# Joined exponentials and moved score groups in a windowed-attention kernel with a ReLU-squared feed-forward behind it

## The chip, the core and the metric

One Trainium2 chip, one of its cores. The metric is the device time of one execution in microseconds (us). TensorE (PE in the profile) multiplies matrices into PSUM, which has eight banks; ScalarE (ACT) evaluates functions, here exponentials, ReLU and copies; VectorE (DVE) works elementwise; GpSimd (POOL) casts and issues loads; SyncE (SP) issues the other transfers. Each engine runs its own instructions in program order and waits on semaphores for the others.

## The reference, cut to what matters

```python
# q, k, v: (8 batch rows, 8 heads, 576 tokens, 64)
rel = pos[:, None] - pos[None, :]
mask_plain = (rel >= 0) & (rel < 32)                      # heads 0 to 3
mask_dil = (rel >= 0) & (rel < 128) & (rel % 4 == 0)      # heads 4 to 7
scores = where(masks, q @ k.T / sqrt(64), -1e9)
attn_out = softmax(scores) @ v
x = attn_out.transpose(0, 2, 1, 3).reshape(4608, 512)
h = x @ w_in            # (512, 2048)
r = maximum(h, 0.0)
out = (r * r) @ w_out   # (2048, 512)
```

## The kernel before

The attention goes by batch row (0 to 7, 576 tokens each), the feed-forward by chunk (0 to 8, 512 tokens each). While the feed-forward of chunk c runs on TensorE, the attention of row c + 1 is strewn between its matmuls. `run` (L861) does this by hand-written plans such as `"7:s34"`: the feed-forward is a generator, `pump(n)` advances it by n steps, and the part named behind the colon is issued after that many steps of the chunk.

A chunk from 2 on has 60 steps. Steps 1 to 32 are the first multiplication and ReLU: 16 tiles with two steps each, a step being two matmuls (L295) of 512 columns, then a ReLU on ACT (L304) and a square on DVE (L329). Steps 33 to 60 are the second multiplication, done for chunks 2 to 8 with seven block products instead of eight (`seven_gen`, L462): four steps for each product, a step being four matmuls (L447) of 256 columns. In this text they are products 1 to 7. Products 1, 2, 3, 5 and 6 end with a copy or sum that takes the result out of its banks: after 3 ACT copies it to `u2` (L514), after each half of 5 to `t7` (L521), after 6 to the output tile (L528). After product 4, DVE computes `S4` in place of S1 (two L433, through `sum_g`), and after product 5 it adds `pc` and `t7` (L523). Product 7 reads S4 and adds on top of `pc`, the banks of product 4. In chunks 0 and 1 the second multiplication is a plain one (L336), two 512-wide matmuls to a step.

The attention of a row has these parts:

- scores in three groups of two kinds each: kinds 0 to 2 are the windowed heads, kinds 3 to 5 the dilated ones. From row 2 on the groups are `s34`, `s50` and `s12` (row 1: `s01`, `s23`, `s45`). A group (`scores`, L641) issues its matmuls (L660, 64 rows by 72 or 96 columns) into two pairs of banks, an exponential of each kind on ACT (L671), and masks on DVE: L675 one mask for a group of two windowed kinds, L682 and L688 one for each kind of the others.
- `a0` to `a2` (windowed) and `d0`, `d1`, `e0`, `e1` (dilated): probabilities times values (L753, L783) into one pair of banks, then a reciprocal and a normalization on DVE (L733, L734).
- `x0`, `x1`, `y0`, `y1`: transposes on TensorE (L805, L820) and copies on ACT into `xr`, the input of the feed-forward (L812, L823). From row 5 on transfers transpose instead; `w0` and `w1` then copy the dilated part into place on ACT (L831).

The pairs are banks 4 and 5 (pair 2) and banks 6 and 7 (pair 3), taken in turn by `pair()` (L84, `turns["pair"]`); the feed-forward uses banks 0 to 3. Each row from 2 on takes an odd number of turns, so the pair on which a row begins alternates. `d0` is the first to take a pair after `s12`.

Chunk 0's second multiplication carries row 1 (L1078). The plans for later rows are `SOON` for the scores, `EARLY` for the rest, and `LATER`, whose second part places the scores of row c + 2 behind chunk c's first multiplication, for c = 3 to 5: `s34` at step 40, `s50` at 47 (behind three quarters of product 4), `s12` at 54 (the middle of product 6). Row 4's groups stand at step 58 of chunk 2 and at steps 2 and 5 of chunk 3, and its `d0` at step 8; row 3's `s12` and `d0` at steps 17 and 21 of chunk 2; row 2's at steps 34 and 40 of chunk 1.

Of the kernel before, what the change touches and what calls it, by code (L numbers as in the profile page):

```python
# [12 lines left out]
ACTF = mybir.ActivationFunctionType  # L13
P = 128
# [3 lines left out]
def kernel(  # L18
# [9 lines left out]
    nc = tc.nc  # L28
# [10 lines left out]
    scale = float(1.0 / (D ** 0.5))  # L39
# [6 lines left out]
    QB = 96  # L46
# [27 lines left out]
    PS = pspool.tile([P, 8, TOKC], FP32, name="PS")  # L74
    turns = {"bank": 0, "pair": 0}
# [8 lines left out]
    def pair(dt=FP32):  # L84
        i = pairs[turns["pair"] % len(pairs)]
        turns["pair"] += 1
        b = PS[:, 2 * i : 2 * i + 2, :]
        return b if dt == FP32 else b.bitcast(dt)
# [36 lines left out]
    AT = const.tile([P, 5120], FP16, name="AT")  # L125
# [7 lines left out]
    maskp = const.tile([P, 2 * 4 * QB], FP16, name="maskp")  # L133
# [23 lines left out]
    def load_whole_sliding_qk(b):  # L157
        n = natp.tile([P, HH, 9, D], FP16, name=f"n{b}", tag="n")
        for i, s in ((1, k), (0, q)):
            nc.gpsimd.dma_start(  # L160
                out=n[64 * i : 64 * (i + 1)],
                in_=s[b, 0:HH].rearrange("h (p j) d -> p h j d", j=9),
            )
        return n
# [85 lines left out]
    def keep_dilated_qk(b):  # L250
        d = dpool.tile([2, HH * CL, DIL * D], FP16, name=f"dd{b}", tag="dd")
        for i, src in ((1, k), (0, q)):
            nc.gpsimd.dma_start(
                out=d[i], in_=src[b, HH:H].rearrange("h (i c) d -> (h i) (c d)", c=DIL)
            )
        return d
# [333 lines left out]
    def t_sliding(b, n, hp):  # L590
        p_ = pair(FP16)
        for i in (1, 0):
            t_sliding_one(b, n, hp, 2 * hp, i, p_[:, i, :])
        for i in (1, 0):
            c_sliding_one(b, hp, i, p_[:, i, :], nc.vector if i else nc.scalar)
# [16 lines left out]
    def t_dilated(b, m, a):  # L612
        p_ = pair(FP16)
        for i in (1, 0):
            t_dilated_one(b, m, a, i, p_[:, i, :])
        for i in (1, 0):
            c_dilated_one(b, a, i, p_[:, i, :], nc.vector if i else nc.scalar)
# [9 lines left out]
    def dilated_of(base, n):  # L627
        return AT[:, base : base + 2 * n * QX].rearrange("p (e n q) -> p e n q", e=2, q=QX)
# [5 lines left out]
    def place_of(block, e):  # L634

        for base, blocks in KINDS:
            if block in blocks:
                w = QB if len(block) == 2 else QX
                return base + w * (e * len(blocks) + blocks.index(block))

    def scores(b, *kinds):  # L641

        tiles = [pair() for i in kinds]
        for i, ps in zip(kinds, tiles):
            for n, block in enumerate(KINDS[i][1]):
                if i < 3:
                    m, hp = block
                    kk = QKTp[b % 2][:, 1, hp, QB * m : QB * m + P]
                    qq = QKTp[b % 2][:, 0, hp, PADP + QB * m : PADP + QB * (m + 1)]
                    w = QB  # L650
                else:
                    t, a, h = block
                    q0 = KPAD + h * CL + QD * t
                    k0 = q0 - (PADE if t else PADD)
                    kk = QKTd[b % 2][:, 1, a, k0 : k0 + P]
                    qq = QKTd[b % 2][:, 0, a, q0 : q0 + QD]
                    w = QD
                for e in range(2):
                    r = slice(D * e, D * (e + 1))
                    nc.tensor.matmul(  # L660
                        ps[:, e, w * n : w * (n + 1)], kk[r], qq[r], start=True, stop=True
                    )
        for i, ps in zip(kinds, tiles):
            base, blocks = KINDS[i]
            n = len(blocks)
            if i < 3:
                to, of = AT[:, base : base + 2 * n * QB], ps[:, :, 0 : n * QB]
            else:
                to = dilated_of(base, n)[:, :, :, 0:QD]
                of = ps[:, :, 0 : n * QD].rearrange("p e (n q) -> p e n q", q=QD)  # L670
            nc.scalar.activation(to, of, ACTF.Exp, scale=scale)  # L671
        if max(kinds) < 3:
            i0, n = kinds[0], len(kinds)
            x = AT[:, 800 * i0 : 800 * (i0 + n)].rearrange("p (i w) -> p i w", w=800)[:, :, 0 : 8 * QB]
            nc.vector.tensor_mul(x, x, maskp.unsqueeze(1).to_broadcast([P, n, 8 * QB]))  # L675
            return
        for i in kinds:
            base, blocks = KINDS[i]
            n = len(blocks)
            if i < 3:  # L680
                x = AT[:, base : base + 2 * n * QB]
                nc.vector.tensor_mul(x, x, maskp)  # L682
                continue

            o = QD * (0, 4, 6)[i - 3]
            mask = maskd.rearrange("p t w -> p (t w)")[:, o : o + n * QD]
            x = dilated_of(base, n)[:, :, :, 0:QD]
            nc.vector.tensor_mul(  # L688
                x,
                x,  # L690
                mask.rearrange("p (n q) -> p n q", q=QD).unsqueeze(1).to_broadcast([P, 2, n, QD]),
            )
# [143 lines left out]
    def row_parts(b, wide):  # L836

        xs, ys, zs = [], [], []
        return {
            "s01": lambda: scores(b, 0, 1),  # L840
            "s23": lambda: scores(b, 2, 3),
            "s45": lambda: scores(b, 4, 5),
            "s34": lambda: scores(b, 3, 4),
            "s50": lambda: scores(b, 5, 0),
            "s12": lambda: scores(b, 1, 2),
            "a0": lambda: av_sliding(b, xs, 0, 1),
            "a1": lambda: av_sliding(b, xs, 2, 3),
            "a2": lambda: av_sliding(b, xs, 4, 5),
            "x0": lambda: b < CROSS and x_sliding(b, 0, xs, wide),
            "x1": lambda: b < CROSS and x_sliding(b, 1, xs, wide),  # L850
            "d0": lambda: av_dilated(b, 0, 0, ys),
            "d1": lambda: av_dilated(b, 0, 1, ys),
            "e0": lambda: av_dilated(b, 1, 0, zs),
            "e1": lambda: av_dilated(b, 1, 1, zs),
            "y0": lambda: b < CROSS and x_dilated(b, 0, ys, wide),
            "y1": lambda: b < CROSS and x_dilated(b, 1, zs, wide),
            "w0": lambda: place_dilated(b, 0),
            "w1": lambda: place_dilated(b, 1),
        }
# [125 lines left out]
    s01 = pair()  # L985
# [18 lines left out]
    for u in (5, 7):  # L1004
        x = AT0[:, u, 0:UW].rearrange("p (e w) -> p e w", e=2)
# [46 lines left out]
    n, dd = load_whole_sliding_qk(2), keep_dilated_qk(2)  # L1052
# [5 lines left out]
    def turn(b, n, dd):  # L1058
# [5 lines left out]
        if b < 4:  # L1064
# [6 lines left out]
        t0=lambda: t_sliding(1, ns1, 0),  # L1071
        t1=lambda: t_sliding(1, ns1, 1),
        u0=lambda: t_dilated(1, nd1, 0),
        u1=lambda: t_dilated(1, nd1, 1),
    )
    run(
        (
            "1:t0 3:t1 6:s01 8:u0 10:u1 12:a0 14:a1 15:s23 17:x0 18:s45 20:a2 22:d0 24:x1"  # L1078
            " 25:d1 26:e0 28:e1 29:y0 30:y1",
            parts,  # L1080
        ),
# [9 lines left out]
    rows_ = {b: row_parts(b, b > SEVEN) for b in range(2, B)}  # L1091
    SOON = "{}:s34 {}:s50 {}:s12"
    EARLY = "{}:d0 {}:d1 {}:e0 {}:y0 {}:e1 {}:a0 {}:y1 {}:a1 {}:a2 {}:x0 {}:x1"
    LATER = (EARLY.format(2, 5, 8, 11, 13, 16, 19, 21, 24, 27, 30), SOON.format(40, 47, 54))
    PLANS = {
        1: (SOON.format(24, 29, 34) + " " + EARLY.format(*range(40, 62, 2)), ""),
        2: (
# [4 lines left out]
            "2:s50 5:s12 " + EARLY.format(8, 11, 14, 17, 19, 22, 24, 27, 30, 33, 36),  # L1102
            LATER[1],
        ),
        4: (LATER[0] + " 57:w0 60:w1", LATER[1]),
        5: (LATER[0] + " 57:w0 60:w1", LATER[1]),
        6: (LATER[0] + " 57:w0 60:w1", ""),
    }

    ORDER = {1: 46, 2: 33, 3: 9, 4: 2, 5: 2}  # L1110
    for c in range(1, NTOKC):
        b = c + 1
# [10 lines left out]
        if b + 1 < B:  # L1123
# [4 lines left out]
            n, dd = load_whole_sliding_qk(b + 1), keep_dilated_qk(b + 1)  # L1128
# [53 lines left out]
```

## Time and profile before

| | |
|---|---|
| runs before | 298.99, 298.40, 298.44 us; median 298.44 |
| profiled execution | 297.93 us, of which 295.6 is the span from first to last instruction |
| TensorE clock granted | full, the whole span |
| VectorE, ScalarE, GpSimd busy | 203.6, 176.5, 97.3 us of the span |
| transfers | DMA engines 9 tenths busy or more in most slices up to about 207 us, 3 tenths or less after it |

The profile shows one execution. Times in its timeline count from the first instruction. Chunk 3 runs from about 120 to 152 us, chunk 4 to 182, chunk 5 to 212; chunks 6 to 8, which carry less and less attention, to 292. Row 1 stands at 36 to 58 us. Matmuls are pipelined: a row "x8" counts eight, its length includes the pipeline's tail of the last one. A weight load (PEld) runs beside the matmul before it. Where an engine stood idle, brackets behind the row give the time and what ended it. "issue" there is time in which the profile shows no wait.

### The profile page before, as it was taken

To read this page: it belongs to the slowest core of one execution; us is meant where nothing else is said; L and a number is where in the kernel's file an instruction comes from. 1 tells how busy PE (TensorE), PEld (TensorE's weight loads), DVE (VectorE), ACT (ScalarE), POOL (GpSimd) and SP (SyncE) were. 2 spreads that over 40 slices of the span, in tenths; PEclk is the share of its full clock that TensorE was granted. 3 is DMA by queue.
4 is the path that set the end of the run, shared out by engine and by line. 5 is a ranking of instruction groups with operands and counts; after the bars stand their busy time and mean duration, and the time that the engine had idled before them with its cause. 6 is when DMAs were issued, how large, how long until landed. Compare 5 with 4: busy or idle time off the path is not lost.

```text
span 295.6 us, 7127 instructions
## 1 busy us (share of the span) xinstructions
PE 285.0 (96%) x2880; PEld 202.5 (69%) x2880; DVE 203.6 (69%) x381; ACT 176.5 (60%) x318; POOL 97.3 (33%) x154
## 2 busy tenths in 40 slices
PE   3989999999999999999999999999999999999995
PEld 2769855565555588557889987568756875785584
DVE  7786656778735997799588958896779524823652
ACT  2678855779438773886645557655756267425711
POOL 8591029406707113951563029309300000000000
PEclk9999999999999999999999999999999999999999
DMA  7999999599899698999999999999223130003013
GB/s 124 240 200 211 213 207 200 160 176 234 161 217 252 140 167 163 237 233 168 205 252 222 175 156 224 240 179 149 79 87 38 26 144 0 0 2 143 2 35 106
DMA packets 73968, 45.58 MB, mean 154 GB/s; under 512 B 56720, under 2 KB 67600, under 8 KB 73744
## 3 DMA queue, kind: packets, MB, share of 16 engines
q1 hardware_dynamic: 66544, 31.37, 48.0%
q0 software_dynamic: 7248, 13.63, 26.0%
q8 instruction: 22, 0.36, 0.5%
q10 hardware_dynamic: 144, 0.13, 0.1%
q14 instruction: 10, 0.08, 0.1%
HBM read 36.83 MB, written 16.52 MB: 180 GB/s over the span
## 4 chain that ended last, share of the span: by engine, by line
PE 83%; DVE 6%; ACT 3%; DMA 3%; issue 2%; SPq 1%; POOL 1%; POOLq 0%; DVEq 0%; ACTq 0%
PE PS L295 40%; PE PS L447 23%; PE PS L336 9%; PE PS L783 2%; PE PS L660 2%; ACT AT L671 2%; DVE S L433 2%; DMA nd<-in_q_dram 2%; PE PS L753 2%; PE PS L577 1%; DMA sv<-in_v_dram 1%; PE PS L805 1%; SPq L172 1%; PE PS L601 1%; PE PS L820 1%
## 5 line engine op out<-in xcount | busy, mean ns | idle before, releaser
L295 PE MATMUL PS<-xr,wi 128*128 128x512 f16 (+3 forms) x704 | 133.3, 341 | 0.3
L304 ACT ACTIVATE rt<-PS 128x512 f16<-128x512 f32 (+2 forms) x160 | 87.9, 557 | 40.8 <-PE PS L295 37.8
L295 PEld LDWEIGHTS <-wi 128*128 128x128 f16 x704 | 75.9, 113 | 38.6 <-issue 0.4
L329 DVE TENSOR_TENSOR g<-rt 128x1024 f16<-128x1024 f16 (+1 forms) x64 | 46.1, 721 | 28.0 <-ACT rt L304 27.6
L447 PEld LDWEIGHTS <-S 128*128 128x128 f16 x448 | 43.0, 98 | 6.4 <-issue 1.1
L671 ACT ACTIVATE AT<-PS 128x768 f16<-128x768 f32 (+2 forms) x42 | 31.8, 810 | 13.7 <-PE PS L660 13.5
L447 PE MATMUL PS<-T,S 128*128 128x256 f16 x336 | 39.0, 273 | 0.0
L447 PEld LDWEIGHTS <-g 128*128 128x128 f16 x336 | 32.3, 98 | 5.1
L336 PE MATMUL PS<-wo,g 128*128 128x512 f16 x128 | 32.9, 379 | 0.0
L239 POOL CAST vd<-sd 128x512 f16<-128x512 f32 x32 | 24.8, 796 | 19.8 <-DMA sd<-in_v_dram 16.7
L222 POOL CAST vp<-sv 128x512 f16<-128x512 f32 x24 | 18.2, 760 | 24.9 <-DMA sv<-in_v_dram 23.8
L447 PE MATMUL PS<-wo,g 128*128 128x256 f16 x224 | 26.3, 273 | 0.0
L688 DVE TENSOR_TENSOR AT<-AT,maskd 128x720 f16<-128x720 f16 (+1 forms) x21 | 14.0, 678 | 14.0 <-ACT AT L671 13.7
L734 DVE TENSOR_TENSOR y<-PS,rcp 72x512 f16<-72x512 f32 (+1 forms) x32 | 22.0, 686 | 1.1
L734 DVE TENSOR_TENSOR x<-PS,rcp 96x512 f16<-96x512 f32 (+1 forms) x25 | 16.6, 665 | 0.9
L783 PEld LDWEIGHTS <-AT 128*128 128x128 f16 x256 | 12.1, 100 | 6.4 <-DVE y L734 1.4
L433 DVE TENSOR_TENSOR S<-g,S 128x1024 f16<-128x1024 f16 x14 | 11.5, 860 | 6.9 <-PE PS L447 6.9
L336 PEld LDWEIGHTS <-g 128*128 128x128 f16 x128 | 10.4, 97 | 8.2
L226 POOL CAST vp<-sv 32x512 f16<-32x512 f32 (+1 forms) x24 | 15.0, 626 | 1.5
L733 DVE RECIPROCAL rcp<-PS 96x8 f32<-96x8 f32 (+3 forms) x57 | 11.2, 197 | 5.4 <-PE PS L753 2.7
L447 PE MATMUL PS<-wo,S 128*128 128x256 f16 x112 | 13.5, 272 | 0.6 <-DVE c L523 0.5
L447 PE MATMUL PS<-T,g 128*128 128x256 f16 x112 | 14.1, 273 | 0.0
(101 smaller groups left out, 287.0 us busy)
## 6 DMA issues: line engine op xcount, KB each, us to landing
out_dram<-c SPq DMA_DIRECT2D x12, 512.0 KB
sv<-in_v_dram SPq DMA_DIRECT2D x48, 96.0 KB, 3.9
sd<-in_v_dram SPq DMA_DIRECT2D x16, 288.0 KB
dp<-o SPq DMA_DIRECT2D x12, 288.0 KB, 3.9
wo<-in_moe_w_out_dram POOLq DMA_DIRECT2D x4, 512.0 KB, 13.9
n<-in_k_dram POOLq DMA_DIRECT2D x6, 288.0 KB, 6.0
n<-in_q_dram POOLq DMA_DIRECT2D x6, 288.0 KB, 6.9
dd<-in_k_dram POOLq DMA_DIRECT2D x6, 288.0 KB, 7.6
```

The costliest lines, as they stand in the source:

```text
L222: nc.gpsimd.tensor_copy(vp[b % 2][:, m : m + 2, :, 0:D], sv[:, m : m + 2, :, :])
L226: nc.gpsimd.tensor_copy(vp[b % 2][0:PADP, m:m1, :, 0:D], sv[P - PADP : P, m - 1 : m1 - 1])
L239: nc.gpsimd.tensor_copy(o, by_class(sd[:, t]))
L295: nc.tensor.matmul(ph[:, o : o + b - a], w_in_of(dmk, ffc), xr[:, dmk, a:b], start=(dmk == 0 and o == 0), stop=(dmk == NDM - 1 and o + b - ...
L304: nc.scalar.activation(rt, ph[:, 0:w], ACTF.Relu)
L329: nc.vector.tensor_mul(g[:, f2 : f2 + 2, o:TOKC], rt[:, :, o:TOKC], rt[:, :, o:TOKC])
L336: nc.tensor.matmul(po, g[:, ffc, o + t * P : o + (t + 1) * P], w_out_of(ffc), start=(ffc == 0), stop=(ffc == NFF - 1),)
L433: nc.vector.tensor_sub(S1[:, f, :], a_of(0, 1, j), S2[:, f, :])
L447: nc.tensor.matmul(po[t], lhs(j)[:, t * P : (t + 1) * P], rhs(j), start=j == 0 and not on_top, stop=j == HF - 1, skip_group_check=on_top,)
L671: nc.scalar.activation(to, of, ACTF.Exp, scale=scale)
L734: nc.vector.tensor_tensor(out=x, in0=pv[:, :, :, 0:D], in1=rcp[0:w, 0:i, 0:j].unsqueeze(3).to_broadcast([w, i, j, D]), op=ALU.mult,)
L783: nc.tensor.matmul(pav[:, e, h * (D + 2) : h * (D + 2) + D + 1], AT[:, off : off + P], vd[b % 2][:, t, 2 * a + e, h, 0 : D + 1], start=Tru ...
```

## The change

Three edits. In `scores`, for groups of windowed kinds from row 2 on (`s12`), the two exponentials of 128 by 768 become one of 128 by 1536 that reads the four banks 4 to 7; before such a group the turn of pairs is made even, so that the group begins on banks 4 and 5, and one turn is skipped where it was odd. The mask behind it is the same instruction as before. In `LATER`, `s50` goes from step 47 to step 45 (the first quarter of product 4 in front of it, three behind it). In row 1's plan `s23`, `x0`, `s45` and `a2` go one step later; `d0`, `x1` and all after them stay. The number of instructions falls by six on ACT and stays on the other engines.

```diff
+    def two_sliding(i):
+        x = AT[:, 800 * i : 800 * (i + 2)].rearrange("p (i w) -> p i w", w=800)
+        return x[:, :, 0 : 8 * QB]
+
     def scores(b, *kinds):
 
+        if b > 1 and max(kinds) < 3:
+
+            turns["pair"] += turns["pair"] % 2
         tiles = [pair() for i in kinds]
...
+        if b > 1 and max(kinds) < 3:
+
+            nc.scalar.activation(
+                two_sliding(kinds[0]).rearrange("p i (e w) -> p i e w", e=2),
+                PS[:, 4:8, 0 : 4 * QB].rearrange("p (i e) w -> p i e w", e=2),
+                ACTF.Exp,
+                scale=scale,
+            )
+            tiles = []
         for i, ps in zip(kinds, tiles):
...
         if max(kinds) < 3:
-            i0, n = kinds[0], len(kinds)
-            x = AT[:, 800 * i0 : 800 * (i0 + n)].rearrange("p (i w) -> p i w", w=800)[:, :, 0 : 8 * QB]
-            nc.vector.tensor_mul(x, x, maskp.unsqueeze(1).to_broadcast([P, n, 8 * QB]))
+            x = two_sliding(kinds[0])
+            nc.vector.tensor_mul(x, x, maskp.unsqueeze(1).to_broadcast([P, 2, 8 * QB]))
             return
...
-            "1:t0 3:t1 6:s01 8:u0 10:u1 12:a0 14:a1 15:s23 17:x0 18:s45 20:a2 22:d0 24:x1"
+            "1:t0 3:t1 6:s01 8:u0 10:u1 12:a0 14:a1 16:s23 18:x0 19:s45 21:a2 22:d0 24:x1"
             " 25:d1 26:e0 28:e1 29:y0 30:y1",
...
-    LATER = (EARLY.format(2, 5, 8, 11, 13, 16, 19, 21, 24, 27, 30), SOON.format(40, 47, 54))
+    LATER = (EARLY.format(2, 5, 8, 11, 13, 16, 19, 21, 24, 27, 30), SOON.format(40, 45, 54))
```

## The prediction

> **What bounds the kernel now.** I read first the page's busy shares and its chain, for the engine that sets the end; then the timelines around each edit, for where that engine stands still.
>
> ```profile
> PE 285.0 (96%) x2880; PEld 202.5 (69%) x2880; DVE 203.6 (69%) x381; ACT 176.5 (60%) x318; POOL 97.3 (33%) x154
> PE 83%; DVE 6%; ACT 3%; DMA 3%; issue 2%; SPq 1%; POOL 1%; POOLq 0%; DVEq 0%; ACTq 0%
> ```
>
> TensorE (PE) is busy for 96% of the span and carries 83% of the chain, so an edit is worth what it takes from PE's standing time, no more. ScalarE (ACT) has 40% of the span free, so its own savings buy nothing by themselves. The largest stop that comes back is one wait per chunk in the second half of chunks 3, 4 and 5. Chunk 4:
>
> ```profile
> 174.14 0.59 ACT L514 COPY u<-PS 128x512 f32<-128x512 f32 x1 [0.46 <-PE PS L447]
> ...
> 175.52 0.34 PE L660 MATMUL PS<-QKTp 64*128 64x96 f16 x8
> 175.73 1.47 ACT L671 ACTIVATE AT<-PS 128x720 f16<-128x720 f32 x2 [1.00 <-PE PS L660]
> 175.79 2.36 PE L447 MATMUL PS<-T,S 128*128 128x256 f16 x20
> ...
> 177.23 0.71 DVE L682 TENSOR_TENSOR AT<-AT,maskp 128x768 f16<-128x768 f16 x1 [0.17 <-ACT AT L671]
> ...
> 177.87 2.11 DVE L433 TENSOR_TENSOR S<-g,S 128x1024 f16<-128x1024 f16 x2
> ...
> 178.18 0.37 ACT L521 COPY t<-PS 128x256 f32<-128x256 f32 x1 [0.50 <-PE PS L447]
> ...
> 178.95 0.51 PE L660 MATMUL PS<-QKTp 64*128 64x96 f16 x16
> 179.34 1.51 ACT L671 ACTIVATE AT<-PS 128x768 f16<-128x768 f32 x2 [0.78 <-PE PS L660]
> ...
> 179.40 1.05 PE L447 MATMUL PS<-T,g 128*128 128x256 f16 x8
> 179.90 0.68 DVE L523 TENSOR_TENSOR c<-PS,t 128x512 f32<-128x512 f32 x1
> ...
> 180.63 1.91 PE L447 MATMUL PS<-wo,S 128*128 128x256 f16 x16 [0.19 <-DVE c L523]
> ...
> 180.74 0.59 ACT L528 COPY c<-PS 128x512 f32<-128x512 f32 x1
> ...
> 181.20 2.49 ACT L831 COPY xr<-xd 128x288 f16<-128x288 f16 x4
> ...
> 182.38 0.81 PE L295 MATMUL PS<-xr,wi 128*128 128x512 f16 x3
> ```
>
> The columns are start, length, engine, work, and in brackets the idle time before it. Twelve more product matmuls (20 against 8) take 2.36 - 1.05 = 1.31 us, 0.109 each. So the second half of product 6, eight from 179.40, is issued by 180.27, and product 7 starts at 180.63: PE stands for 0.36. Backwards: product 7 adds onto the banks that VectorE (DVE) L523 reads, and L523 ends at 180.58; it is queued behind S4 (the two L433, 2.11 us), and these stand right behind the mask of s50 (L682, to 177.94), whose exponentials ACT began at 175.73. L523's other input, the second L521 copy, is there at 178.55, and product 4, which S4 must let finish, is through its last four matmuls (of the 175.79 row) by about 176.4. So s50's place sets the start of product 7. The other two chunks:
>
> ```profile
> 149.47 1.05 PE L447 MATMUL PS<-T,g 128*128 128x256 f16 x8
> ...
> 150.62 1.91 PE L447 MATMUL PS<-wo,S 128*128 128x256 f16 x16
> ```
>
> ```profile
> 209.25 1.05 PE L447 MATMUL PS<-T,g 128*128 128x256 f16 x8
> ...
> 210.61 1.91 PE L447 MATMUL PS<-wo,S 128*128 128x256 f16 x16 [0.31 <-DVE c L523]
> ```
>
> By the same eight matmuls (0.87): 150.62 - 150.34 = 0.28 and 210.61 - 210.12 = 0.49. The three stops are 1.13 us.
>
> **s50 two steps sooner.** Two steps of a product are eight matmuls, 0.87 us. What moves with it are 18 small matmuls, two exponentials and two masks; it issues no DMA and passes no step that does, so neither SyncE's nor GpSimd's queue changes. Its ACT work could begin at 174.86, and ACT is free at 174.73 (the u2 copy L514). The mask then ends at 177.07, S4 at about 179.1, L523 at 179.8, and PE arrives at 180.27: nearly 0.5 us to spare, in chunk 5, where the stop is larger than here by 0.13, still 0.35. All three stops go: **-1.13**. Its cover is DVE: were S4 and the masks to take 0.4 us longer than now, the stop would begin to come back. Bounds: -1.13 (there is no more) and -0.5, if half is lost to a slower DVE.
>
> **Row 1 a step later.** In chunk 0's second multiplication the scores s23, x0, s45 and a2 are put one step back, d0 and the rest stay.
>
> ```profile
> 46.25 0.69 DVE L734 TENSOR_TENSOR x<-PS,rcp 96x512 f16<-96x512 f32 x1
> 46.27 0.34 PE L660 MATMUL PS<-QKTp 64*128 64x96 f16 x8
> ...
> 46.65 1.63 ACT L671 ACTIVATE AT<-PS 128x768 f16<-128x768 f32 x2 [2.42 <-PE PS L660]
> 46.99 0.37 PE L660 MATMUL PS<-QKTd 64*128 64x72 f16 x12 [0.37 <-DVE x L734]
> ...
> 48.62 0.70 ACT L812 COPY xr<-PS 128x288 f16<-128x288 f16 x2 [0.34 <-PE PS L805]
> ...
> 49.33 1.43 ACT L671 ACTIVATE AT<-PS 128x720 f16<-128x720 f32 x2
> ...
> 50.13 1.80 DVE L688 TENSOR_TENSOR AT<-AT,maskd 128x720 f16<-128x720 f16 x2 [1.14 <-ACT AT L671]
> ...
> 52.92 0.69 DVE L734 TENSOR_TENSOR y<-PS,rcp 72x512 f16<-72x512 f32 x1
> ...
> 53.66 0.30 PEld L783 LDWEIGHTS <-AT 128*128 128x128 f16 x8 [0.48 <-DVE y L734]
> ```
>
> s23 comes too early: its first eight matmuls are issued by about 46.45, the rest wait until 46.99 for a1's normalization (L734, to 46.94), 0.54 us. A step later two 512-wide matmuls (0.43) fill that hole, so PE is 0.43 ahead in work by 47.3. But s23's exponentials then run from 47.08 instead of 46.65, end at 48.71 instead of 48.28, and the x0 copies (L812), which could start at 48.62, start at 48.71: 0.09 late. s45's second half waits for them, so its exponentials (49.33) and masks (50.13) follow 0.09 late, and from 50.13 to 53.61 DVE has no hole: 1.80 of masks and 2 x 0.69 for the normalizations of a2 and d0 (52.92) leave 0.3 of these 3.48 us for their two reciprocals. d1 needs d0's pair and waits for DVE already, as the last row says. So d1 starts at about 53.75 instead of 53.67, and the 0.43 won before is spent waiting there: **+0.08**. Bounds: -0.54 if DVE keeps up, +0.2 if ACT and DVE each add such a 0.09 of their own. I take the end to which the unbroken DVE queue points.
>
> **One exponential over four banks.** It stands in for two in rows 2 to 7. No row shows such an instruction; the nearest:
>
> ```profile
> L671 ACT ACTIVATE AT<-PS 128x768 f16<-128x768 f32 x21 | 16.3, 812 | 6.1 <-PE PS L660 6.0
> L263 ACT COPY o<-n 128x1536 f16<-128x1536 f16 x3 | 4.4, 1478 | 1.6 <-DMA n<-in_q_dram 1.1 <-ACT rt L304 0.5
> ```
>
> An ACT copy of the same 1536 columns takes 1.48 us, a pair of 768-wide exponentials 1.51 (row of 179.34; they overlap a little, 2 x 0.81 = 1.62). I take 1.47; bounds 1.36 (a tenth under the pair) and 1.62 (nothing shared). ACT's busy time hardly falls, by 0.04 six times, and it is not the bound. But the one instruction waits for all 16 matmuls. The first of the two started after eight, and the other eight cost PE 0.17 (16 take 0.51, row of 178.95, eight take 0.34, row of 175.52). So it ends 0.17 + 1.47 - 1.51 = 0.13 later than the pair, and both bank pairs are held until then. The skipped pair matters too: for rows 3 to 7 the group starts on banks 4 and 5.
>
> Who waits? Row 4, in chunk 3, where s50, s12 and d0 stand three steps apart:
>
> ```profile
> 121.51 1.47 ACT L671 ACTIVATE AT<-PS 128x720 f16<-128x720 f32 x2
> ...
> 122.71 0.67 PE L660 MATMUL PS<-QKTp 64*128 64x96 f16 x16
> ...
> 123.33 1.54 ACT L671 ACTIVATE AT<-PS 128x768 f16<-128x768 f32 x2
> ...
> 124.63 0.42 PE L783 MATMUL PS<-vd,AT 128*128 128x65 f16 x8
> ...
> 124.91 1.20 DVE L675 TENSOR_TENSOR AT<-AT,maskp 128x1536 f16<-128x1536 f16 x1
> ...
> 128.01 0.31 PEld L783 LDWEIGHTS <-AT 128*128 128x128 f16 x8 [0.59 <-DVE y L734]
> ```
>
> s50's second exponential ends at 122.98. So far only the second half of s12 needs its banks and waits to about 123.03, which is why its 16 matmuls take 0.67 here and not 0.51. In the changed kernel these are banks 4 and 5, where the first half goes, so all 16 run from 123.03, and the exponential starts 0.38 (as at s23, 46.27 to 46.65) + 0.17 later, at 123.58, and ends at 125.05 instead of 124.87. d0 (124.63), on banks 4 and 5 again, must wait for it, to 125.1, 0.47 late. But PE stands before e0 so far too (0.59 us between weight loads at 128.01, some 0.3 of it a stop of the matmuls, for d0's normalization L734), and what decides e0 is the mask L675 and DVE's queue behind it, now 0.18 later: PE's delay of 0.47, less the 0.3 it no longer stands, comes to the same. **+0.20** in round numbers. Bounds: 0 (if DVE runs its queue tighter) and +0.5 (d0's whole delay). Row 3, in chunk 2:
>
> ```profile
> 97.45 1.51 ACT L671 ACTIVATE AT<-PS 128x768 f16<-128x768 f32 x2
> ...
> 99.26 0.42 PE L783 MATMUL PS<-vd,AT 128*128 128x65 f16 x8
> ```
>
> The exponential ends at 97.45 + 0.17 + 1.47 = 99.09 and d0 starts at 99.26: free, with 0.1 to spare. Row 2's d0 is six steps behind, free. In chunks 4 and 5 (rows 6 and 7) the copy L528 and the four copies L831 stand behind the exponential on ACT. L831's second copy, which the fourth matmul of the next chunk's first tile reads, ends near 181.20 + 2 x 0.62 + 0.1 = 182.54, then 182.67; PE comes there at 182.38 - 0.36 + 3 x 0.21 = 182.65. The margin is used up, with perhaps 0.05 to wait; I take the same for chunk 5: **+0.1** for both, bounds 0 and +0.4. In chunk 3 row 5 has no such copies: free.
>
> Sum: -1.13 + 0.08 + 0.20 + 0.10 = **-0.75 us**.
>
> The Trainium skill speaks against this edit: "Perfetto Trace Analysis", section "Optimizing Scalar/DVE Operations", says to group operations where the engine is saturated and to break them up where it is not but makes other engines wait. ACT's 60% makes this the second case. The trace bears it out at row 4, whose d0 follows too soon, and not at row 3, where 0.1 is to spare; if it held everywhere, all six joins would cost, which is rival (a).
>
> **Rivals.** (a) *Every join costs.* If each of the six delays is passed on, 6 x 0.18 = 1.1 stands in place of 0.30, and the sum is 0.0: 298.5. For it, the thin margins of row 3 and of L831; against it, d0 six steps off in row 2 and a whole chunk start off in chunk 3. (b) *Row 1 pays.* If DVE catches up behind s45, 0.54 is won instead of 0.08 lost: -1.37, 297.1. For it, GpSimd's casts that run beside those masks could move; against it, the DVE queue without a hole. (c) *The wait before product 7 only shrinks*, because the masks and S4, moved, meet other GpSimd work and slow down: half of 1.13, sum -0.2, 298.3. Against it, 0.35 to 0.5 us in hand. (d) *Slower: the four-bank exponential is long.* Place: row 4's d0 and e0 and the L831 copies of chunks 4 and 5, three places without margin, and row 3 from 0.1 on. Each 0.1 us over 1.47 costs 0.3, later 0.4. Break-even is near 1.7 us, slower by 0.6 us near 1.85; at 1.9 the sum is 3 x 0.43 + 0.33 - 0.75 = +0.9, 299.3. For it, no row shows a read of four banks; against it, the 1.48 us copy of the same length.
>
> **How the numbers follow.** The profiled execution took 297.93 us, 295.6 of it span; nothing outside the span is touched, so 297.18 by it. The median shown is 298.44, 0.51 above that execution, and the time I forecast is against the median: 298.44 - 0.75 = 297.7. A measurement of this kernel tells no less than 0.2%, 0.6 us, from no change, so the forecast is just past that line. Chances: forecast 0.48 (0.35 of it past 0.6 us, 0.13 short), (a) 0.12, (b) 0.16, (c) 0.10, (d) 0.14. Faster 0.35 + 0.16 = 0.51; same 0.13 + 0.12 + 0.10 = 0.35; slower 0.14. Range 297.0 to 298.6: from (b) to (a), leaving out (d) and little else; the forecast's own is 297.3 to 298.1.
>
> **What would show it.** Right: in chunks 3, 4 and 5 S4 starts about 0.87 us sooner against its chunk, and product 7 follows product 6 without a stop; s23's matmuls run through, but d1 still waits for d0's normalization at about 53.7; the exponential takes 1.45 to 1.5 us; row 4's d0 waits for ACT, and e0 starts about 0.2 later against its chunk. Wrong: product 7 still waits for L523; row 1 ends by more than 0.3 earlier; the exponential takes 1.6 us or more, or matmuls of the next chunk wait for L831 by more than 0.1.

## The result, and the profile after

| | before | after |
|---|---|---|
| median of seven runs each, us | 298.40 (297.86 to 298.99) | 296.98 (296.42 to 297.61) |
| ratio, 95% interval | | 0.9954 [0.9935, 0.9973] |
| profiled execution / its span, us | 297.93 / 295.6 | 296.72 / 294.7 |

By the ratio the change saves 0.46%, 1.37 us, with an interval from 0.8 to 1.9. Forecast were 0.75 us and 297.7, in a range from 297.0 up: what came lies at its lower end (the median 0.02 us under it; by the ratio, against the 298.44 from which the forecast was made, 297.07). Of the executions that follow, one, the profiled one of s50_only, ran at a granted TensorE clock of 0.57 and took 490 us; the times and traces below leave it out.

The busy shares of the changed kernel and the engines' parts of its chain:

```profile
PE 285.1 (97%) x2880; PEld 203.1 (69%) x2880; DVE 203.0 (69%) x381; ACT 175.8 (60%) x312; POOL 99.5 (34%) x154
...
PE 90%; ACT 3%; DMA 3%; DVE 2%; POOL 1%; issue 1%; POOLq 0%; ACTq 0%
```

TensorE's work is what it was, 285 us. VectorE's part of the chain falls from 6% to 2% between these two executions: waits on it are what went. Chunk 4 in the timeline (columns: start, length, engine, work, idle time before it):

```profile
176.76 1.29 DVE L433 TENSOR_TENSOR S<-g,S 128x1024 f16<-128x1024 f16 x2
...
178.18 1.75 POOL L239 CAST vd<-sd 128x512 f16<-128x512 f32 x3
178.51 0.69 DVE L523 TENSOR_TENSOR c<-PS,t 128x512 f32<-128x512 f32 x1 [0.47 <-ACT t L521]
...
179.32 1.05 PE L447 MATMUL PS<-T,g 128*128 128x256 f16 x8
179.43 1.45 ACT L672 ACTIVATE AT<-PS 128x1536 f16<-128x1536 f32 x1 [0.95 <-PE PS L667]
...
180.21 1.91 PE L447 MATMUL PS<-wo,S 128*128 128x256 f16 x16
...
181.25 2.49 ACT L846 COPY xr<-xd 128x288 f16<-128x288 f16 x4
...
181.96 1.04 PE L295 MATMUL PS<-xr,wi 128*128 128x512 f16 x4
```

Product 6's second half, eight matmuls from 179.32, is issued by 180.19 (eight by the prediction's 0.109), and product 7 begins at 180.21: no stop, and no bracket. In this chunk L523 waits no longer for its place in VectorE's queue but for ACT's copy L521, and is through at 179.20, 1.0 us before it is needed. The prediction had half of that; the rest is that S4's two L433 took 1.29 us here, with no cast of GpSimd beside them (the first starts at 178.18), and not 2.11. The other two stops are gone as well; chunks 3 and 5:

```profile
149.66 1.05 PE L447 MATMUL PS<-T,g 128*128 128x256 f16 x8
...
150.54 1.91 PE L447 MATMUL PS<-wo,S 128*128 128x256 f16 x16
...
208.84 1.05 PE L447 MATMUL PS<-T,g 128*128 128x256 f16 x8
...
209.73 1.91 PE L447 MATMUL PS<-wo,S 128*128 128x256 f16 x16
```

Row 1:

```profile
45.97 0.42 PE L768 MATMUL PS<-vp,AT 128*128 128x65 f16 x8
...
47.18 0.34 PE L667 MATMUL PS<-QKTp 64*128 64x96 f16 x8
47.47 0.37 PE L667 MATMUL PS<-QKTd 64*128 64x72 f16 x12
...
49.10 0.70 ACT L827 COPY xr<-PS 128x288 f16<-128x288 f16 x2
...
50.61 1.58 DVE L703 TENSOR_TENSOR AT<-AT,maskd 128x720 f16<-128x720 f16 x2 [0.69 <-ACT AT L687]
...
53.17 0.69 DVE L749 TENSOR_TENSOR y<-PS,rcp 72x512 f16<-72x512 f32 x1
...
53.91 0.31 PEld L798 LDWEIGHTS <-AT 128*128 128x128 f16 x8 [0.48 <-DVE y L749]
```

s23's two halves no longer have the bracket between them, and d1 still waits for d0's normalization (last row), as it did. From a1 (45.97, the first row) to d1's first matmul are 7.95 us, against 8.18 before. That looks like a gain of the moved groups; it is not one, as the experiments show.

Row 4, where the joined exponential delays d0:

```profile
119.89 1.03 PE L295 MATMUL PS<-xr,wi 128*128 128x512 f16 x4
...
123.03 0.52 PE L667 MATMUL PS<-QKTp 64*128 64x96 f16 x16 [0.25 <-ACT AT L687]
123.58 1.45 ACT L672 ACTIVATE AT<-PS 128x1536 f16<-128x1536 f32 x1
...
125.08 0.31 PEld L798 LDWEIGHTS <-AT 128*128 128x128 f16 x8 [0.60 <-ACT AT L672]
...
128.22 0.31 PEld L798 LDWEIGHTS <-AT 128*128 128x128 f16 x8 [0.33 <-DVE y L749]
```

All 16 score matmuls now wait for s50's exponential, the joined one runs from 123.58, and d0's weight load at 125.08 waits for it for 0.60 us. Its first matmul comes 5.20 us after the chunk's start, 4.74 before; e0's 8.33 after it, 8.12 before. It is the only place where TensorE waits for a joined exponential: the group of all these weight loads (columns: busy time, mean ns; idle time before them by what ended it) has waited for L672 for 0.6 us in all.

```profile
L798 PEld LDWEIGHTS <-AT 128*128 128x128 f16 x256 | 12.0, 100 | 6.6 <-DVE y L749 1.2 <-ACT AT L672 0.6 <-DVE g L329 0.2
```

Where the span's 0.9 us went, by place, that is, by how far the same matmuls have moved between the two traces: the feed-forward matmuls start 0.48 later from the first one on (at 18.9 us in before, in front of all edits), row 1 gives 0.23 back, a stop at 112 us for a cast of GpSimd, which only the traces of before and row4_split have, gives 0.25; row 4 costs 0.21, and the stops before product 7 give 0.27, 0.35 and 0.47: +0.48 - 0.23 - 0.25 + 0.21 - 1.09 = -0.88. Of these only the last two terms are the work of the edits, as the experiments show. For the other five joined exponentials nothing is left.

### The profile page after: what moved, and what is told of

It is laid out like the page before. It is cut to its first block, busy times and chain, and to the rows that moved or that the text cites. A ratio compares the mean times of both kernels' runs of the same rounds, so it can differ in the third digit from the quotient of the medians.

```text
span 294.7 us, 7121 instructions
## 1 busy us (share of the span) xinstructions
PE 285.1 (97%) x2880; PEld 203.1 (69%) x2880; DVE 203.0 (69%) x381; ACT 175.8 (60%) x312; POOL 99.5 (34%) x154
## 4 chain that ended last, share of the span: by engine, by line
PE 90%; ACT 3%; DMA 3%; DVE 2%; POOL 1%; issue 1%; POOLq 0%; ACTq 0%
PE PS L295 41%; PE PS L447 29%; PE PS L336 8%; PE PS L667 3%; PE PS L798 3%; DMA ns<-in_q_dram 3%; PE PS L768 2%; ACT AT L687 1%; PE PS L835 1%; PE PS L820 1%; PE PS L577 1%; DVE x L749 1%; DVE AT L703 1%; ACT AT L672 0%; ACT xr L827 0%
## 5 line engine op out<-in xcount | busy, mean ns | idle before, releaser
L239 POOL CAST vd<-sd 128x512 f16<-128x512 f32 x32 | 23.6, 760 | 24.4 <-PE PS L447 14.7
L687 ACT ACTIVATE AT<-PS 128x720 f16<-128x720 f32 (+2 forms) x30 | 22.7, 809 | 8.9 <-PE PS L667 8.4
L226 POOL CAST vp<-sv 32x512 f16<-32x512 f32 (+1 forms) x24 | 17.4, 724 | 1.5
L433 DVE TENSOR_TENSOR S<-g,S 128x1024 f16<-128x1024 f16 x14 | 10.5, 787 | 6.9 <-PE PS L447 6.9
L521 ACT COPY t<-PS 128x256 f32<-128x256 f32 x14 | 5.2, 374 | 14.6 <-PE PS L447 14.6
```

What stands on the lines that cost most here:

```text
L226: nc.gpsimd.tensor_copy(vp[b % 2][0:PADP, m:m1, :, 0:D], sv[P - PADP : P, m - 1 : m1 - 1])
L239: nc.gpsimd.tensor_copy(o, by_class(sd[:, t]))
```

## The experiments

### Each edit alone

Row 1's plan alone, the moved s50 alone, and the joined exponential alone:

```diff
 # row1_only: before, with
-            "1:t0 3:t1 6:s01 8:u0 10:u1 12:a0 14:a1 15:s23 17:x0 18:s45 20:a2 22:d0 24:x1"
+            "1:t0 3:t1 6:s01 8:u0 10:u1 12:a0 14:a1 16:s23 18:x0 19:s45 21:a2 22:d0 24:x1"
 # s50_only: before, with
-SOON.format(40, 47, 54)
+SOON.format(40, 45, 54)
 # join_only: after, with step 47 and the old plan of row 1
 # no_join: both moves, two exponentials as before
```

> The kernel before with s50 alone two steps sooner (step 45) in the plans of chunks 3 to 5; two exponentials and row 1's steps as before. Theory A (the gain is the three stops before product 7): product 7 follows product 6 without a stop in chunks 3, 4 and 5, 1.10 to 1.13 us less than before, nothing else moves; time about 1.1 us under the kernel before, ratio 0.9963. Rival B (most of the gain comes from row 1 or from the joined exponential): 0.5 us or less under it, the stops at least in part still there.

> The kernel before with row 1's four parts alone one step later. Theory A (DVE's queue behind s45's masks hides it): the 0.54 us stop inside s23 goes, but d1 still waits for d0's normalization and starts within 0.1 us of its old distance from a1; total within 0.2 us of the kernel before. Rival B (row 1 pays): d1 stands 0.25 us or more nearer to a1, total 0.25 to 0.5 us less.

> The kernel before with the one exponential over four banks alone. Theory A: one exponential takes 1.45 us, row 4's d0 waits for it and e0 stands 0.2 us later against the start of chunk 3; the three stops before product 7 are as before; total 0.2 us slower, or within the noise of that. Rival B (the join helps, and the total gain of 1.4 us holds a part of it): total 0.2 us or more faster, with row 4's e0 no later.

> Both moves (s50 two steps sooner, row 1 one step later) and two exponentials as in the kernel before. Theory A: row 4's e0 is 0.2 us sooner than in the changed kernel, so the time is 0.2 us under the changed kernel's, 1.3 to 1.6 us under the kernel before. Rival B (the join helps): slower than the changed kernel, 1.1 us or less under the kernel before.

| | ratio to before, 95% interval | median, us (before: 297.77) |
|---|---|---|
| s50_only | 0.9967 [0.9943, 0.9990] | 297.06 |
| row1_only | 0.9998 [0.9974, 1.0023] | 298.02 |
| join_only | 1.0004 [0.9980, 1.0028] | 298.14 |
| no_join | 0.9949 [0.9927, 0.9971] | 296.66 |

Of the three edits only s50's gives a time that can be told from no change, about 1.0 us (0.3 to 1.7). The two others are each within 0.3% of nothing, in both directions. With both moves and without the join the time is that of the full change; their intervals overlap. The trace of s50_only is a second one, s50_only_again.

The profile of row1_only has the old s50, and larger stops before product 7 than before has itself, 0.68, 1.67 and 0.27 us. (It is the slowest of that kernel's twelve executions, 300.30 us against a median of 298.02.) The first mask of s50 in chunk 4 of before, while GpSimd casts nothing:

```profile
176.53 0.53 DVE L688 TENSOR_TENSOR AT<-AT,maskd 128x720 f16<-128x720 f16 x1 [2.28 <-ACT AT L671]
```

Chunk 4 in row1_only:

```profile
177.63 1.84 DVE L688 TENSOR_TENSOR AT<-AT,maskd 128x720 f16<-128x720 f16 x1 [2.28 <-ACT AT L671]
177.88 2.07 POOL L239 CAST vd<-sd 128x512 f16<-128x512 f32 x3
...
179.40 0.96 DVE L682 TENSOR_TENSOR AT<-AT,maskp 128x768 f16<-128x768 f16 x1
...
180.28 2.11 DVE L433 TENSOR_TENSOR S<-g,S 128x1024 f16<-128x1024 f16 x2
...
180.50 1.05 PE L447 MATMUL PS<-T,g 128*128 128x256 f16 x8
...
182.31 0.68 DVE L523 TENSOR_TENSOR c<-PS,t 128x512 f32<-128x512 f32 x1
...
183.04 1.91 PE L447 MATMUL PS<-wo,S 128*128 128x256 f16 x16 [1.50 <-DVE c L523]
```

The same mask takes 1.84, and in that time two casts of GpSimd run through and a third begins. All behind it on VectorE is late by that: S4, L523, product 7. This is no single case: in the thirteen traces used here this mask took 0.52 to 0.54 us in all 57 places with no cast beside it, and 0.52 to 1.84 in the 120 that shared more than 0.1 us with casts. So the stop is not a fixed 0.36 us, it depends on where GpSimd is in its list when the masks come.

### The stops, with s50 a step sooner, two steps sooner, and its masks doubled

```diff
 # s50_one_step: before, with
-SOON.format(40, 47, 54)
+SOON.format(40, 46, 54)
 # masks_twice: no_join (step 45), with s50's two masks in rows 5 to 7 applied twice
-                nc.vector.tensor_mul(x, x, maskp)
+                for again in range(1 + (b > 4)):
+                    nc.vector.tensor_mul(x, x, maskp)
...
-            nc.vector.tensor_mul(
+            for again in range(1 + (b > 4 and kinds[0] == 5)):
+                nc.vector.tensor_mul(
...
 # before_again, s50_only_again, after_again: a second profile of the same kernel
```

> The kernel before with s50 one step sooner (46) instead of two: 0.44 us. Theory A (a stop shrinks by as much as s50 moves, down to nothing): stops of 0.28 and 0.36 us go, of the third some 0.05 us is left, about 1.0 us under the kernel before in a quiet execution; where GpSimd's casts stretch the masks, stops come back. Rival B (two steps are needed): two or three stops of 0.2 us or more are left.

> Both moves and two exponentials as in no_join, and s50's two masks of rows 5 to 7 applied twice (they are zeros and ones, so the values stay): 1.1 to 1.9 us more VectorE work ahead of S4 in chunks 3, 4 and 5, nothing more on TensorE. Theory A (VectorE's queue from s50's masks to L523 sets the start of product 7): the 0.35 to 0.8 us that no_join has in hand there are used up, and stops of 0.5 to 1.4 us come back in each of the three chunks, 2 to 3.5 us in all, time 298.7 to 300.2. Rival B (something else let product 7 go, the masks do not matter): no stop, time as no_join within 0.4 us.

> The kernel before once more, for a second execution's stops. Theory A (the three stops are steady, 1.1 us in all): 0.28, 0.36 and 0.49 us again within 0.1 each. Rival B (they vary with where GpSimd's work falls beside VectorE's masks and sums): their sum differs from 1.1 us by 0.3 us or more.

> s50 alone two steps sooner, for its profile at full clock. Theory A: no stop before product 7 in chunks 3, 4 and 5, row 4's e0 within 0.15 us of its distance from the start of chunk 3 before, row 1 as before. Rival B: a stop of 0.2 us or more is left.

> The changed kernel once more. Theory A: no stop before product 7 again; row 4's d0 waits for the exponential and e0 stands 0.15 to 0.25 us later against the start of chunk 3 than in the kernel before; in row 1 the distance from a1 to d1 is 7.9 to 8.2 us, by GpSimd's phase. Rival B: one of the three differs by more than 0.2 us from the first profile.

| | ratio to before, 95% interval | median, us (before: 298.23) |
|---|---|---|
| s50_one_step | 0.9946 [0.9925, 0.9968] | 296.80 |
| masks_twice | 1.0063 [1.0028, 1.0099] | 300.05 |

The three with one execution each took 297.71 (before_again), 297.56 (s50_only_again) and 296.67 us (after_again); a single time says little, and what counts of them are the traces. The stops before product 7 (its first matmul, less the last of product 6, less 0.107 for that one), in us:

| s50 at step | kernel | chunk 3 | chunk 4 | chunk 5 | sum |
|---|---|---|---|---|---|
| 47 | before | 0.27 | 0.35 | 0.48 | 1.10 |
| 47 | before_again | 0.48 | 0.36 | 0.50 | 1.34 |
| 47 | join_only | 0.34 | 0.43 | 0.49 | 1.26 |
| 47 | row1_only | 0.68 | 1.67 | 0.27 | 2.62 |
| 46 | s50_one_step | 0.16 | 0 | 0 | 0.16 |
| 45 | after, after_again, no_join, row4_split | 0 | 0 | 0 | 0 |
| 45 | s50_only_again | 0 | 0.86 | 0 | 0.86 |
| 45 | masks_twice | 0.73 | 1.62 | 0.74 | 3.09 |

before_again lies between its two theories: 0.21 us more in chunk 3, 0.24 in the sum. after_again came as its theory A says (e0 8.31 us behind the start of chunk 3, 8.18 from a1 to d1), s50_only_again has a stop left, as its rival B says.

At step 47 the four profiles have a mean of 1.58, at 45 the five without doubled masks 0.17: 1.4 us by place. But 1.58 leans on row1_only, the longest of twelve executions; the other three have a mean of 1.23, which makes it 1.1. Already one step gives nearly all of it. What is left at step 46, in chunk 3:

```profile
147.25 2.11 DVE L433 TENSOR_TENSOR S<-g,S 128x1024 f16<-128x1024 f16 x2
...
148.98 1.05 PE L447 MATMUL PS<-T,g 128*128 128x256 f16 x8
149.28 0.68 DVE L523 TENSOR_TENSOR c<-PS,t 128x512 f32<-128x512 f32 x1
...
150.02 1.91 PE L447 MATMUL PS<-wo,S 128*128 128x256 f16 x16
```

L523 ends at 149.96, product 6 is issued by 149.85, product 7 starts at 150.02. Here S4 took its 2.11 us and one step was just too little. The doubled masks bring the stop back with the second step too; chunk 4:

```profile
178.20 1.79 DVE L690 TENSOR_TENSOR AT<-AT,maskd 128x720 f16<-128x720 f16 x2 [1.41 <-ACT AT L671]
...
179.92 1.84 DVE L683 TENSOR_TENSOR AT<-AT,maskp 128x768 f16<-128x768 f16 x2
...
181.68 2.11 DVE L433 TENSOR_TENSOR S<-g,S 128x1024 f16<-128x1024 f16 x2
...
181.94 1.05 PE L447 MATMUL PS<-T,g 128*128 128x256 f16 x8
...
184.44 1.91 PE L447 MATMUL PS<-wo,S 128*128 128x256 f16 x16 [1.45 <-DVE c L523]
```

The four masks and S4 stand in one unbroken queue from 178.20 to 183.8, and TensorE stands 1.62 us for L523 behind it, a little more than the 1.4 expected for one chunk. The three chunks together stand 3.09 us, within the 2 to 3.5 expected. That is nearly the 3.4 us by which masks_twice is slower than no_join (each against its own before: 1.0063 and 0.9949), though the profiled execution, 301.66 us, is itself 1.6 over the median; its trace has one more stop, 2.05 us at 138.7, behind a cast of GpSimd (L226) that took 1.98 us where 0.61 is usual. And S4 alone can do it; s50_only_again, chunk 4:

```profile
176.47 3.65 DVE L433 TENSOR_TENSOR S<-g,S 128x1024 f16<-128x1024 f16 x2
176.79 1.75 POOL L239 CAST vd<-sd 128x512 f16<-128x512 f32 x3
...
179.03 1.05 PE L447 MATMUL PS<-T,g 128*128 128x256 f16 x8
...
180.04 0.68 DVE L523 TENSOR_TENSOR c<-PS,t 128x512 f32<-128x512 f32 x1
...
180.78 1.47 PE L447 MATMUL PS<-wo,S 128*128 128x256 f16 x12 [0.69 <-DVE c L523]
```

S4 starts in time and takes 3.65 us, 1.54 longer than the 2.11 of before. Product 6 is issued by 179.90, product 7 begins at 180.78. That is Rival (c), in one chunk of the fifteen that were seen at step 45. In the fourteen others L523 is through 0.3 to 1.0 us before product 6 is issued.

### The joined exponential, by place

```diff
 # row4_split: after, but row 4 keeps two exponentials; in both places
-        if b > 1 and max(kinds) < 3:
+        if b > 1 and b != 4 and max(kinds) < 3:
```

> The changed kernel with two exponentials again in row 4 alone. Theory A (the join costs in row 4 alone, 0.2 us there): e0 of row 4 stands 0.1 to 0.2 us nearer to the start of chunk 3 than in the changed kernel, time 0.2 us under it, as no_join within noise. Rival B (the join is worth something in row 4 too): slower than the changed kernel.

The time is 296.58, ratio 0.9952 [0.9934, 0.9971]: not told apart from the full change by time. By place it is. With two exponentials d0 stands 4.73 or 4.74 us behind the start of chunk 3 in every profile, with the joined one 5.20. e0 stands 8.14 us behind it in the mean of eight profiles with two (7.84 to 8.37), 8.32 in the mean of three with one (8.31 to 8.33): +0.2, a difference of means (row4_split itself has 8.04, s50_one_step 8.37). Row 4 of no_join, to be read against that of after above:

```profile
119.85 1.03 PE L295 MATMUL PS<-xr,wi 128*128 128x512 f16 x4
...
124.58 0.42 PE L783 MATMUL PS<-vd,AT 128*128 128x65 f16 x8
...
124.86 1.29 DVE L675 TENSOR_TENSOR AT<-AT,maskp 128x1536 f16<-128x1536 f16 x1
...
128.07 0.43 PE L783 MATMUL PS<-vd,AT 128*128 128x65 f16 x8 [0.21 <-DVE y L734]
```

d0 at 124.58 does not wait, and e0 at 128.07 waits for the normalization. With the joined exponential d0 waits instead, and then the matmuls go into e0 without a stop in all three traces (the bracket at 128.22 above is that of the weight load alone). With two, e0 stands at 7.84 where VectorE does not hold it up (before_again) and at up to 8.37 where it does, by stops of 0.2 to 0.5 us. So the join costs 0.47 us less the stop that falls away: in a given execution anything from 0.47 to nothing, 0.2 in the mean.

### Row 1 with GpSimd's casts out of the way

Row 1's masks of s45 take 1.58 to 1.80 us, and GpSimd's casts run beside them. To take the casts away from there, they were put ahead of the loads of row 2 in GpSimd's order, with the old and with the new plan of row 1:

```diff
 # casts_first_old: before; casts_first_new: row1_only; in chunk 0
-    n, dd = load_whole_sliding_qk(2), keep_dilated_qk(2)
     cast_sliding_v(1, 2)
     for t in range(2):
         for a in range(2):
             cast_dilated_v(1, t, a)
+    n, dd = load_whole_sliding_qk(2), keep_dilated_qk(2)
```

> The kernel before with GpSimd's order in row 1 changed: the casts of row 1's last values stand ahead of the loads for row 2 instead of behind them, so that they run before s45's masks and not beside them (row 2's loads are issued some 5 us later, and what that costs further on is not of interest here). Row 1's plan as before. Theory A (GpSimd's casts beside them stretch s45's masks, 1.6 to 1.8 us for two of 0.53 to 0.7, and so d0's normalization and d1): the two masks take 1.2 to 1.4 us, and from a1's matmuls to d1's it is 7.9 to 8.0 us instead of 8.18. Rival B (the masks are as long without the casts): 1.6 us or more, 8.18 us.

> The same order on GpSimd with row 1's four parts one step later. Theory A (DVE's queue behind s45's masks alone keeps the 0.43 us of the step from counting): with the masks at 1.2 to 1.4 us the distance from a1 to d1 falls to 7.6 to 7.8 us, below that of casts_first_old by 0.15 us or more. Rival B (ACT's chain through s23's exponentials and x0's copies keeps it): within 0.05 us of casts_first_old.

Both did another thing than they were made for: 306.01 and 305.95 us in one execution each, where before took 299.06. Two of the casts still ran beside the masks (49.87 and 50.55 in the old plan), which took 1.63 and 1.69, and row 2's loads now came late. Then VectorE's copy of them, which stands in its queue ahead of a normalization, held the queue; old plan:

```profile
60.03 0.55 DVE L265 COPY o<-n 128x768 f16<-128x768 f16 x1 [6.63 <-DMA n<-in_q_dram]
...
61.47 0.62 PE L783 MATMUL PS<-vd,AT 128*128 128x65 f16 x8 [6.04 <-DVE y L734]
```

In none of these traces do row 1's masks of s45 run without a cast beside them, so how long they would take there without one stays open (elsewhere the same mask takes 0.52 to 0.54, as said). But the pair still compares the two plans: 8.00 us from a1 to d1 with the old, 8.05 with the new. (Both have s50 at step 47; their stops before product 7 add up to 1.18 and 1.86.) All other profiles, in us:

| plan of row 1 | a1 to d1 |
|---|---|
| old: before, before_again, join_only, s50_one_step, s50_only_again | 8.18, 8.18, 8.19, 7.96, 7.96 |
| new: after, after_again, row1_only, no_join, row4_split, masks_twice | 7.95, 8.18, 8.16, 7.95, 8.17, 7.96 |

Both plans have the same two values, 7.96 and 8.18. The second profile of the changed kernel has the longer one:

```profile
45.52 0.41 PE L768 MATMUL PS<-vp,AT 128*128 128x65 f16 x8
...
50.17 1.80 DVE L703 TENSOR_TENSOR AT<-AT,maskd 128x720 f16<-128x720 f16 x2 [0.47 <-ACT AT L687]
...
53.70 0.43 PE L798 MATMUL PS<-vd,AT 128*128 128x65 f16 x8
```

The masks begin about 4.65 us after a1 in each (50.61 - 45.97, 50.17 - 45.52, and 50.13 - 45.49 before) and take 1.58 or 1.80. The 0.22 between these is the 0.23 between the two values of d1. The plan moves neither.

## Why the prediction was right, and where it was off

**s50, the mechanism.** Right. The chain from s50's masks through S4 and L523 to product 7 was read off one trace, and every link answers: sooner masks, no stop; masks twice, 3.09 us of stops; a longer S4, 0.86. "About 0.87 us sooner" and "without a stop" both came: in chunks 3, 4 and 5 S4 starts 0.75, 1.03 and 0.86 us sooner against its chunk's first matmul. The cover that the prediction named, VectorE with 0.35 to 0.5 us in hand, is the real one (0.3 to 1.0 in fourteen chunks of fifteen): one step less leaves 0.16 in one chunk of three, and S4 longer by 1.54 uses it up.

**s50, the size.** -1.13 was the sum of three stops of one execution, with the remark that there is no more to be had. That was a bound of this execution, not of the kernel: it has the smallest sum of the six at step 47. With row 1's old plan the four are 1.10, 1.34, 1.26 and 1.18, a mean of 1.22; with the new plan the two are 2.62 and 1.86, and all six have a mean of 1.56. On average 0.17 returns at step 45. So the term is somewhere from -1.1 to -1.4. Whether the new plan itself makes these stops larger, two profiles cannot show; the time of row1_only, 0.9998 of before, speaks against a lasting effect.

**Row 1.** That VectorE's queue behind s45 swallows what TensorE wins in s23's hole was right: d0 stands 5.72 us behind a1 instead of 6.14, and TensorE then waits before x1 and d1. The +0.08 was not: s23's second half stands 1.50 us behind a1 before and after (46.99 - 45.49, 47.47 - 45.97), since it waited for a1's normalization anyway, and the copies L827 start 3.13 behind it as L812 did (48.62 - 45.49, 49.10 - 45.97). The supposed delay of 0.09 came from adding the pair's 1.63 to a start 0.43 later and letting the copies begin only then; the pair took 1.59 there (to 49.15), and the copies' record begins 0.05 before its end. The term is 0.00. Rival (b), 0.54 won, falls, although its sum, -1.37, is the very number that was measured: that is chance.

**The joined exponential.** Its duration was forecast as 1.47 us; the group has six of 1.45. Rival (d) falls with that, and nothing of four banks shows in it. Row 4 came out link by link up to d0: exponential from 123.58 (forecast 123.58), d0 0.46 late (0.47). For e0 the prediction gave two reckonings that agree, VectorE's queue 0.18 later, and TensorE's 0.47 less the 0.3 that it no longer stands. The second is what the traces show: with the join e0 does not wait. That the cost was 0.2 hangs on the size of the stop before, 0.28 in the trace that was read and 0 to 0.53 in others, so the close number holds luck. In the other rows TensorE never waits for the exponential, so rival (a) falls. Also the +0.1 for the copies before chunks 5 and 6 was not there: in the rows of chunk 4 above, the next chunk's first four matmuls go through in 1.04 us, without a bracket. The 0.13 by which the copies were to come later did come: they start 181.25 - 179.32 = 1.93 behind product 6's second half, 181.20 - 179.40 = 1.80 before. But the margin held, barely: in this trace the second copy ends at 182.56 and the fourth matmul starts at 182.62. Chunk 6's first four take 1.03.

The sum, with the terms as measured by place: -1.1 to -1.4, + 0.0 + 0.2 + 0.0, is -0.9 to -1.2 us, against -1.37 with an interval of 0.56 to either side. Forecast were -0.75. Of the difference 0.18 is two small losses, 0.08 for row 1 and 0.1 for the copies, that were each charged for a used-up margin and did not occur; up to 0.27 is the stops; the rest lies within the interval. The sign and the place were right.

**Which version is best** stays open: without the join, or with the join everywhere but in row 4, the 0.2 us of row 4 are saved by place, but the ratios (0.9949 and 0.9952, against 0.9954 for the change) lie closer together than their intervals are wide.

## What to carry to other kernels

A stop that hangs on another engine's queue can change its size from execution to execution; price its removal from several profiles, since one gives only one draw, and the smallest of six here was less than half of the largest. When work is moved ahead of such a stop, ask for the slack in terms of the longest duration that the queue's operations ever show (here S4: 1.29 to 3.65 us, most often 2.11), not of their usual one. A hole closed on the bounding engine is worth nothing where that engine waits for another queue a little later, and an instruction that joins two costs only where its consumer follows within the time by which it ends later (one place of six here), and there only what is not taken out of a wait that stood behind it anyway.

## What was not expected of the hardware

The same VectorE instruction takes very different times beside GpSimd's casts. S4's two L433 took 1.29 us in after's chunk 4, with no cast beside them, 1.70 to 2.11 in most chunks where casts ran beside them, and 3.65 in s50_only_again, where the first of the two lasted 2.63, while three casts passed in 1.75 us (row of 176.79 there), 0.58 each. A single L433 took 0.68 or 0.69 in all 114 places without a cast. The first of the two in s50_only_again:

```profile
176.47 2.63 DVE L433 TENSOR_TENSOR S<-g,S 128x1024 f16<-128x1024 f16 x1
```

A mask of 0.53 us took 1.84 beside casts in row1_only, and casts can be long too: 1.98 instead of 0.61 us in masks_twice. The Trainium skill, "SBUF — State Buffer", section "Who interferes with whom", says that a VectorE instruction with two SBUF inputs (the masks and L433 are such) contends with a GpSimd instruction that reads SBUF, that the ports which the two share are an exclusive lock, and that the order of issue decides which of them blocks. The trace agrees that they get in each other's way, but not with one wait for one cast: by the durations here that would have made this L433 about 0.6 + 0.68 us long, and it took 2.63, about three casts and itself. By the records it had even started first, at 176.47 against 176.79 for the casts (GpSimd was issuing a load until then). What decides the order between them no run here shows.
